# Sink rows on SP's queue and a later sink transposition in a windowed attention plus MLP mixer kernel

## The chip, the cores and the metric

The kernel runs on one core of one Trainium2 chip. The metric is device time in microseconds, the median of several runs: 228.32 us before the change (3 runs, 228.24 to 228.4).

## The reference

The first part is attention with sink tokens and a sliding window, over 4 batches, 8 heads, 768 positions and a head dimension of 64. Position `s` sees the first 4 keys (the sink rows) and the last 128 keys up to itself:

```
scores = scale * np.matmul(q, k.transpose(0, 1, 3, 2))
keep = is_sink | in_window          # pos < n_sink, or 0 <= rel < window
a = softmax(np.where(keep, scores, -1e9))
x = np.matmul(a, v)                 # heads joined to 512 channels
```

The second part is an MLP mixer over the result, first across tokens, then across channels:

```
h = np.maximum(xt @ w_tok1, 0.0) @ w_tok2     # xt: x with tokens last
u = x + h.transpose(0, 2, 1)
h2 = np.maximum(u @ w_ch1, 0.0) @ w_ch2
return u + h2
```

Inputs and output are float32. The kernel computes in bf16 with f32 accumulation.

## The kernel before

Heads are worked in pairs, 16 pairs in all, four to a batch. `load_qk` (L66) loads q and k of one pair in float32 with two DMAs on SP's queue, 384 KB each. `load_v` (L98) loads v of one pair with one DMA on POOL's queue that casts to bf16. `load_w` (L125) loads the weights on POOL's queue with a cast: `w_tok1`, `w_tok2`, and `w_ch1` and `w_ch2` in four parts each ("ch1" and "ch2" below).

For each pair the stages are these:

- `cast_qk` (L89) or, from pair 4 on, `cast` (L756) turn q and k into bf16 on POOL. Pair 0 is cast on DVE and ACT.
- `transpose_q` and `transpose_k` transpose on PE with six matmuls each (L111); the evictions to `qT` and to `kTz`, the two heads of k with zeros in the other half, go to DVE or ACT (L115, L117).
- `score(p, kt)`, six units of a pair, multiplies one block of 128 keys with two blocks of queries into PSUM, after a matmul that adds the mask (in batch 0). ACT takes the exponential (L438). For pair 0 each unit has one more matmul that only keeps TensorE busy (`keep_warm`).
- `score_sinks` does the same for the 4 sink rows, whose keys are in `kTs`, and `pv(p, half)` multiplies the probabilities with v and with the sink rows of v (`v_sink`). DVE takes the reciprocal of the sums (L491) and normalises into `x_sb` (L494).

Token mixing (`mix_h`, `mix_u`, `transpose_u`) follows each batch of four pairs, then channel mixing (`mix_channels`: `v1` units with `w_ch1`, `out_part` units with `w_ch2`).

Every instruction is issued in the order of the program, engine by engine (`in_order`), and an engine that waits at one instruction holds back what follows it. The order of the first stage is written by hand: SP issues q and k of pairs 0 to 3 (L130), and POOL issues, between L179 and L198, v of pair 0, the two sink loads of k, v of pair 1, the two sink loads of v, then the casts of pairs 1 and 2, v of pairs 2 and 3, the casts of pair 3, `w_tok1`, `w_tok2`, v of pair 4, the four parts of ch1 and v of pair 5 (L218 to L225). q and k of pair 4 wait on SP until `w_tok1` has landed, those of pair 5 until the second part of ch1 has landed.

The sink rows of batch 0 are loaded for all four pairs at once, one DMA for each head of the pairs (16 rows of 64 elements, 2 KB in bf16), into tiles that DVE has set to zero before; DVE also sets the column of ones of `v_sink` at the sink rows. `transpose_sinks` transposes `k_sink` on PE into `kTs`. It is the first unit behind `transpose_k` of pair 0. For later batches the sink rows come from `kTz` and `v`.

The order of everything else is set by `Plan.run` while the program is built. It keeps a clock for each engine, gives each unit a cost and each load a due time (the table `LANDED`, L765; for later loads the cost of a "Q" operation, that begins with 36500 ns, L778), and at each step appends the operation that can begin first. A main list (batch 0's attention, then the channel mixing of each batch) and a side list (the attention of the next batch) share PE. The casts of pair 4 and later, the loads of pair 6 and later (`load_pair`) and the loads of ch2 (`load_w2`) are placed by this plan too. `load_pair` and `load_w2` hand on `held`, the last load on POOL's queue: q and k of pairs 6 and 7 wait on SP until it has landed.

Of the kernel before, what the change touches and what calls it, by code (L numbers as in the profile page):

```python
# [9 lines left out]
FP32 = mybir.dt.float32  # L10
# [6 lines left out]
def kernel(  # L17
# [13 lines left out]
    nc = tc.nc  # L31
    B, H, S, D = q.shape
    P = 128
# [7 lines left out]
    NHP = H // 2  # L41
    HS = S // 2
    D1 = D + 1
    scale = 1.0 / float(D) ** 0.5

    singles = ctx.enter_context(tc.tile_pool(name="singles", bufs=1))
# [14 lines left out]
    in_order = tc.keep_in_program_order  # L61
# [4 lines left out]
    def load_qk(pidx, first=None):  # L66
        b, hp = pairs[pidx]
        h0 = 2 * hp
        raw = []
        for t, name in ((q, "q_f"), (k, "k_f")):  # L70
            f = raw_pool.tile([P, 2, NT, D], FP32, name=name)
            d = in_order(nc.sync.dma_start(
                out=f.rearrange("p h j d -> p h (j d)"),
                in_=t[b, h0:h0 + 2].rearrange("h (p j) d -> p h (j d)", j=NT),
            ))
            if first is not None:
                tc.add_manual_dep(
                    d.ins, first.ins.name,
                    mybir.DependencyInfo(mybir.DependencyClass.Sync, mybir.DependencyReason.DATA),
                    reason="transfers in the order in which they are needed",  # L80
                )
            raw.append(f)
        return raw
# [14 lines left out]
    def load_v(pidx):  # L98
        b, hp = pairs[pidx]
        v_aug = v_buf[pidx % NV]  # L100
        d = in_order(nc.gpsimd.dma_start(  # L101
            out=v_aug.rearrange("p i t d -> p (i t) d")[:, :, 0:D],
            in_=v[b].rearrange("h s d -> (h s) d")[2 * hp * S:2 * (hp + 1) * S].rearrange("(n p) d -> p n d", p=P),
        ))
        return v_aug, d
# [7 lines left out]
    def copy(e, out, in_):  # L113
        if e == "ACT":
            in_order(nc.scalar.activation(out, in_, AF.Copy))  # L115
        else:
            in_order({"DVE": nc.vector, "POOL": nc.gpsimd}[e].tensor_copy(out=out, in_=in_))  # L117
# [7 lines left out]
    def load_w(out, in_):  # L125
        return in_order(nc.gpsimd.dma_start(out=out, in_=in_))

    done = {}
    tiles = {}
    raws = {pidx: load_qk(pidx) for pidx in range(NHP)}  # L130
    vs = {}


# [3 lines left out]
    def keep_warm(n):  # L137
# [15 lines left out]
        out=ident, in_=ident, compare_op=ALU.not_equal, fill=1.0, base=0, pattern=[[-1, P]], channel_multiplier=1,  # L153
    ))
    for i in range(2):
        in_order(nc.gpsimd.affine_select(  # L156
            out=mask_main[:, i, 0], in_=mask_main[:, i, 0], compare_op=ALU.is_ge,
# [15 lines left out]
    v_sink0 = singles.tile([P, NHP, 2, D1], BF16, name="v_sink")  # L173
    v_sinks = [v_sink0[:, n] for n in range(NHP)]

    k_sink0 = singles.tile([P, NHP, 2, D], BF16, name="k_sink")
    in_order(nc.vector.memset(k_sink0, 0.0))
    in_order(nc.vector.memset(v_sink0, 0.0))
    vs[0], _ = load_v(0)  # L179
    for i in range(2):  # L180
        rows = slice(D * i, D * i + n_sink)
        in_order(nc.gpsimd.dma_start(  # L182
            out=k_sink0[rows, :, i], in_=k[0].rearrange("(p i) s d -> i s p d", i=2)[i, 0:n_sink],
        ))
    vs[1], _ = load_v(1)
    for i in range(2):
        rows = slice(D * i, D * i + n_sink)
        in_order(nc.vector.memset(v_sink0[rows, :, i, D:D1], 1.0))
        in_order(nc.gpsimd.dma_start(
            out=v_sink0[rows, :, i, 0:D], in_=v[0].rearrange("(p i) s d -> i s p d", i=2)[i, 0:n_sink],  # L190
        ))
    in_order(nc.vector.memset(kTz[0][D:P, 0], 0.0))
    in_order(nc.vector.memset(kTz[0][0:D, 1], 0.0))
    bfs = {0: cast_tiles()}
    cast_qk(1)
    cast_qk(2)
    vs[2], _ = load_v(2)
    vs[3], _ = load_v(3)  # L198

    w_tok1 = singles.tile([P, NT, DTOK], BF16)  # L200
# [15 lines left out]


    cast_qk(3)  # L218
    tok1_landed = load_w(w_tok1, moe_w_tok1.rearrange("(t p) n -> p t n", p=P))
    load_w(w_tok2, moe_w_tok2.rearrange("(t p) n -> p t n", p=P))  # L220
    raws[NHP] = load_qk(NHP, tok1_landed)
    vs[NHP], _ = load_v(NHP)
    ch1_landed = [load_ch1(n) for n in range(NW)]
    raws[NHP + 1] = load_qk(NHP + 1, ch1_landed[1])
# [18 lines left out]
    def landed(at):  # L243
        op = Op({}, None)
        op.done = at
        return op
# [92 lines left out]
    def unit(ns, fn, deps=(), tag=None, then=(), readers=None):  # L339
        op = Op({"PE": float(ns)}, fn, deps, tag, then, size=float(ns))  # L340
        for f in then:
            if op not in f.deps:
                f.deps.append(op)
        op.readers = list(then) if readers is None else readers
        return op
# [3 lines left out]
    def transpose_q(p):  # L349
        key = ("qT", p)  # L350

        def run():
            tiles["ps_q", p] = bank("mx", NT, P, dtype=BF16)
            for j in range(NT):
                transpose(tiles["ps_q", p][:, j], bfs[p][0][:, j])
            if p == 0:
                keep_warm(3)

        def evict(e):
            t = att_pool.tile([P, P, NT], BF16, name="qT2")  # L360
            copy(e, t, tiles["ps_q", p].rearrange("d j p -> d p j"))
            tiles[key] = t.rearrange("d p j -> d (p j)")

        done[key] = Op({"DVE": 950.0, "ACT": 900.0}, evict)
        done["tq", p] = unit(340, run, [done["q_bf", p]], "mx", [done[key]])
        return done["tq", p]
# [35 lines left out]
    def transpose_sinks():  # L402
        def run():
            ps = tiles["ps_ks"] = bank("mx", NHP, P, dtype=BF16)
            for n in range(NHP):
                transpose(ps[:, n], k_sink0[:, n].rearrange("p i d -> p (i d)"))

        op = Op({"ACT": 590.0, "DVE": 420.0}, lambda e: copy(e, kTs0.rearrange("p n i d -> p n (i d)"), tiles["ps_ks"]))
        for n in range(NHP):
            done["kTs", n] = op  # L410
        return unit(224, run, [landed(8000.0)], "mx", [op])

    def score(p, kt):
        nq = 2 if kt < NT - 1 else 1
# [222 lines left out]

    def attention_and_tokens(b):
        p0 = b * NHP
        units = [transpose_sinks()] if b == 0 else []  # L640
        units = [transpose_q(p0), transpose_k(p0)] + units
        for p in range(p0, p0 + NHP):
            more = p < p0 + NHP - 1
            units += [score(p, 0), score(p, 1)]
            if more:
                units.append(transpose_q(p + 1))
            if p > p0:
                units.append(pv(p - 1, 0))
            units += [score(p, 2), score(p, 3)]
            if more:  # L650
                units.append(transpose_k(p + 1))
            units.append(score(p, 4))
            if p > p0:
                units.append(pv(p - 1, 1))
            units += [score(p, 5), score_sinks(p)]

            if b:
                units[-1].then.append(sink_rows(p))
            if b and p == p0 + 2:
                units.append(mix_h(b, 0, 0, NTOK))  # L660
                units += [mix_u(b, 0, st, 2) for st in range(0, NT, 2)]
                plan.pending.append(transfer_u(b, 0, 0, NT, range(0, NT, 2)))
        if b == 0:
            units += [mix_h(b, 0, 0, 1), pv(p, 0), mix_h(b, 0, 1, 1), pv(p, 1)]
            units += [mix_u(b, 0, 0, 1, True), mix_u(b, 0, 1, 1), mix_h(b, 1, 0, NTOK), mix_u(b, 0, 2, 1, True)]
            units += [transpose_u(b, 0, 0, 1), mix_u(b, 0, 3, 1), transpose_u(b, 0, 1, 1)]
            units += [mix_u(b, 1, 0, 4), mix_u(b, 0, 4, 1, True), transpose_u(b, 0, 2, 1), mix_u(b, 1, 4, 2)]
            units += [mix_u(b, 0, 5, 1), transpose_u(b, 0, 3, 1), transpose_u(b, 0, 4, 1)]
            units += [transpose_u(b, 1, 0, 4), transpose_u(b, 1, 4, 2), transpose_u(b, 0, 5, 1)]
        else:  # L670
            units += [pv(p, 0), pv(p, 1), mix_h(b, 1, 0, NTOK)]
            units += [mix_u(b, 1, st, 2) for st in range(0, NT, 2)]
            plan.pending += [transfer_u(b, 1, 0, 4, (0, 2)), transfer_u(b, 1, 4, 2, (4,))]
        return units
# [81 lines left out]
    def cast(n, i, name):  # L756
# [7 lines left out]

    LANDED = {  # L765
        "q_bf": [0, 8400, 10500, 14700], "k_bf": [0, 9500, 12000, 15500],
        "v": [14700, 16300, 17800, 19200, 25000, 35500], "vs": [9500] * NHP,
        "raw": [0] * NHP + [26000, 36500],
    }
    for n in LANDED:  # L770
        for p in range(len(LANDED[n])):
            done[n, p] = landed(float(LANDED[n][p]))
    done["tok1"], done["tok2"] = landed(21100.0), landed(23000.0)
    for n in range(NW):
        done["ch1", n] = landed(27500.0 + 2000.0 * n)

    plan = Plan()
    plan.free.update(PE=3000.0, ACT=2200.0, DVE=3900.0, Q=36500.0)  # L778
# [15 lines left out]
    def pad_rest(e):  # L794
        in_order(nc.vector.memset(kTz[1][D:P, 0], 0.0))
        in_order(nc.vector.memset(kTz[1][0:D, 1], 0.0))

    done["masks"] = Op({"DVE": 1000.0}, mask_rest, [landed(4400.0)])
    done["pads"] = Op({"DVE": 760.0}, pad_rest, [done["k_bf", 0]])
    plan.pending += [done["masks"], done["pads"]]  # L800

    for n in range(NHP, len(pairs)):
        if n >= NHP + 2:
# [74 lines left out]
```

## Time and profile before

| | |
|---|---|
| median of 3 runs | 228.32 us (228.24 to 228.4) |
| the profiled execution | 229.29 us, of which the span is 227.6 us |
| mean granted clock of TensorE | 0.974 |
| PE, DVE, ACT, POOL busy | 93%, 57%, 51%, 23% of the span |
| DMA moved | 28.60 MB, mean 126 GB/s |

The profile was taken of one execution. All its times are counted from the start of the span. PE is TensorE, PEld its loading of weights, DVE the vector engine, ACT the scalar engine, POOL GpSimd and SP the engine that issues most DMAs. A line of a timeline gives the start, the duration, the engine, the line of the code, the operation, the tile written and the tile read, and in brackets how long the engine was idle before it and what ended that. A line of the chain gives the start and the length of one link of the chain of work that ended last, followed back from the last instruction. A line of the waits view gives who waited for whom, the microseconds in total, the number of times and the longest. "Landing" is the time from the issue of a DMA to its last byte.

### The profile page before, as it was taken

To read this page: it belongs to the slowest core of one execution; us is meant where nothing else is said; L and a number is where in the kernel's file an instruction comes from. 1 tells how busy PE (TensorE), PEld (TensorE's weight loads), DVE (VectorE), ACT (ScalarE), POOL (GpSimd) and SP (SyncE) were. 2 spreads that over 40 slices of the span, in tenths; PEclk is the share of its full clock that TensorE was granted. 3 is DMA by queue.
4 is the path that set the end of the run, shared out by engine and by line. 5 is a ranking of instruction groups with operands and counts; after the bars stand their busy time and mean duration, and the time that the engine had idled before them with its cause. 6 is when DMAs were issued, how large, how long until landed. Compare 5 with 4: busy or idle time off the path is not lost.

```text
span 227.6 us, 4342 instructions
## 1 busy us (share of the span) xinstructions
PE 210.6 (93%) x1738; PEld 135.6 (60%) x1756; DVE 130.3 (57%) x285; ACT 117.0 (51%) x233; POOL 52.5 (23%) x70
## 2 busy tenths in 40 slices
PE   7419989999999999999999999999999999999992
PEld 2216667777676665577766565567766654665440
DVE  7302776859866935379996735599939452000321
ACT  3304888689875710397891600689966110774000
POOL 7799023470474140230332000000000000000000
PEclk9956999999999999999999999999999999999998
DMA  6999999999999599480325514200003224100222
GB/s 182 322 172 152 224 226 182 209 157 169 313 347 132 122 287 196 156 277 5 25 16 57 137 50 108 99 4 0 3 0 70 94 78 129 49 0 0 92 92 94
DMA packets 51604, 28.60 MB, mean 126 GB/s; under 512 B 35712, under 2 KB 48512, under 8 KB 51584
## 3 DMA queue, kind: packets, MB, share of 16 engines
q0 software_dynamic: 29920, 7.09, 33.3%
q1 hardware_dynamic: 21664, 21.24, 30.2%
q8 instruction: 13, 0.21, 0.4%
q14 instruction: 7, 0.06, 0.1%
HBM read 26.76 MB, written 6.29 MB: 145 GB/s over the span
## 4 chain that ended last, share of the span: by engine, by line
PE 83%; DMA 5%; DVE 5%; ACT 3%; issue 2%; POOL 1%; ACTq 0%
PE ps_mx L108 64%; PE ps_sc L108 9%; PE ps_pv L108 5%; DMA k_sink<-in_k_dram 5%; PE ps_mx L111 5%; DVE kTz L117 2%; ACT kTz L115 1%; ACT pT L438 1%; DVE o_sb L710 1%; DVE x_sb L494 0%; POOL v_aug L101 0%; DVE qT L117 0%; DVE kTs L117 0%; POOL k_sink L182 0%; POOL mask_main L156 0%
## 5 line engine op out<-in xcount | busy, mean ns | idle before, releaser
L108 PE MATMUL ps_mx<-uT,w_ch 128*128 128x384 bf16 x384 | 69.8, 326 | 0.1
L108 PE MATMUL ps_mx<-w_ch,v1T 128*128 128x512 bf16 x274 | 65.0, 379 | 0.7
L438 ACT ACTIVATE pT<-ps_sc 128x512 bf16<-128x512 f32 x84 | 45.8, 567 | 24.1 <-PE ps_sc L108 23.1
L108 PEld LDWEIGHTS <-w_ch 128*128 128x128 bf16 x384 | 36.8, 98 | 20.8
L710 DVE TENSOR_TENSOR o_sb<-ps_mx,u_sb 128x512 f32<-128x512 f32 x24 | 16.5, 688 | 49.3 <-PE ps_mx L108 47.4
L108 PEld LDWEIGHTS <-v1T 128*128 128x128 bf16 x288 | 27.5, 98 | 28.5
L121 ACT ACTIVATE v1T<-ps_mx 128x384 bf16<-128x384 f32 x67 | 32.8, 491 | 18.1 <-DVE o_sb L710 9.8
L108 PE MATMUL ps_sc<-qT,kTz 128*128 128x256 bf16 x168 | 29.6, 268 | 2.3 <-DVE kTz L117 0.9
L444 DVE TENSOR_TENSOR pT<-pT,mask_main 128x512 bf16<-128x512 bf16 (+1 forms) x59 | 26.3, 457 | 1.0 <-ACT pT L438 0.5
L108 PEld LDWEIGHTS <-kTz 128*128 128x128 bf16 x192 | 17.8, 99 | 12.7 <-issue 2.0
L101 POOL DMA_DIRECT2D v_aug<-in_v_dram x16 | 16.6, 1039 | 23.9 <-PE ps_sc L108 12.0
L108 PEld LDWEIGHTS <-w_tok 128*128 128x128 bf16 x192 | 17.7, 98 | 5.6 <-issue 0.5
L123 DVE TENSOR_SCALAR v1T<-ps_mx 128x384 bf16<-128x384 f32 x29 | 16.0, 556 | 5.5 <-PE ps_mx L108 5.2
L117 POOL CAST q_bf<-q_f 128x768 bf16<-128x768 f32 x12 | 10.0, 830 | 36.8 <-DMA q_f<-in_q_dram 15.5
L117 DVE COPY qT<-ps_mx 128x768 bf16<-128x768 bf16 x13 | 12.4, 955 | 10.2 <-PE ps_mx L111 10.1
L108 PEld LDWEIGHTS <-pT 128*128 128x128 bf16 x352 | 16.8, 98 | 1.9
L595 DVE TENSOR_TENSOR u_sb<-ps_mx,x_sb 128x512 bf16<-128x512 f32 (+2 forms) x23 | 14.0, 655 | 6.3 <-PE ps_mx L108 6.2
L121 ACT ACTIVATE h1T<-ps_mx 128x512 bf16<-128x512 f32 (+2 forms) x9 | 4.9, 549 | 22.9 <-PE ps_mx L108 22.9
L115 ACT ACTIVATE kTz<-ps_mx 64x768 bf16<-64x768 bf16 x19 | 15.2, 801 | 2.6 <-PE ps_mx L111 1.8
L108 PE MATMUL ps_pv<-v_aug,pT 128*128 128x65 bf16 x304 | 16.2, 194 | 0.0
L494 DVE TENSOR_TENSOR x_sb<-ps_pv,recip 128x384 bf16<-128x384 f32 x28 | 15.5, 554 | 0.5
L117 DVE COPY kTz<-ps_mx 64x768 bf16<-64x768 bf16 x13 | 12.4, 955 | 1.7 <-PE ps_mx L111 1.3
(71 smaller groups left out, 198.3 us busy)
## 6 DMA issues: line engine op xcount, KB each, us to landing
q_f<-in_q_dram SPq DMA_DIRECT2D x16, 384.0 KB, 5.8
k_f<-in_k_dram SPq DMA_DIRECT2D x16, 384.0 KB, 6.4
out_dram<-o_sb SPq DMA_DIRECT2D x24, 256.0 KB, 2.0
v_aug<-in_v_dram POOLq DMA_DIRECT2D x16, 192.0 KB, 6.8
w_ch<-in_moe_w_ch_dram POOLq DMA_DIRECT2D x8, 384.0 KB, 8.7
w_tok<-in_moe_w_tok_dram POOLq DMA_DIRECT2D x2, 384.0 KB, 5.7
uT<-u_sb SPq DMA_TRANSPOSE x9, 3.2
k_sink<-in_k_dram POOLq DMA_DIRECT2D x2, 2.0 KB, 11.2
```

What stands on the lines that cost most here:

```text
L101: d = in_order(nc.gpsimd.dma_start(out=v_aug.rearrange("p i t d -> p (i t) d")[:, :, 0:D], in_=v[b].rearrange("h s d -> (h s) d")[2 * hp * ...
L108: in_order(nc.tensor.matmul(*args, skip_group_check=True, **kwargs))
L111: in_order(nc.tensor.transpose(out, in_, ident))
L115: in_order(nc.scalar.activation(out, in_, AF.Copy))
L117: in_order({"DVE": nc.vector, "POOL": nc.gpsimd}[e].tensor_copy(out=out, in_=in_))
L121: in_order(nc.scalar.activation(out, in_, AF.Relu))
L123: in_order(nc.vector.tensor_scalar_max(out=out, in0=in_, scalar1=0.0))
L438: in_order(nc.scalar.activation(tiles["pT", p][:, kt, :, 0:nq], tiles["ps_s", p, kt][:, :, 0:nq * P], AF.Exp, scale=scale,))
L444: in_order(nc.vector.tensor_tensor(out=pt, in0=pt, in1=msk[:, :, 0:nq], op=ALU.mult))
L494: in_order(nc.vector.tensor_tensor(out=x_sb[b][:, ts(half, QH), ts(hp, 2 * D)].rearrange("p t (i d) -> p t i d", i=2), in0=tiles["ps_o", p ...
L595: in_order(nc.vector.tensor_tensor(out=u_part(b, g, s0, n), in0=tiles["ps_u", b, g, s0], in1=x_sb[b][:, s0:s0 + n, c0:c0 + cn], op=ALU.add,))
L710: in_order(nc.vector.tensor_tensor(out=o_sb.rearrange("p (g c) -> p g c", g=2), in1=u_rows(b, st), in0=tiles["ps_out", b, st].rearrange("p ...
```

## The change

The sink rows are loaded in float32 on SP's queue. Two float32 tiles, `k_sink_f` and `v_sink_f`, are set to zero by DVE; the two loads of k's sink rows stand between the loads of q and k of pair 0 and those of pair 1, and the two loads of v's sink rows between pair 1 and pair 2. The ones of v's tile are set by DVE behind each of v's loads. Two new operations, placed by the plan on DVE or ACT, cast the tiles to bf16. POOL no longer issues sink loads. The unit `transpose_sinks` stands behind the fourth score unit of pair 0, just ahead of `transpose_k` of pair 1. The loads of q and k of pair 4 wait for v of pair 2 and no longer for `w_tok1`. Some due times of the plan are changed.

```diff
-    raws = {pidx: load_qk(pidx) for pidx in range(NHP)}
+    raws = {0: load_qk(0)}
...
+    sinks_f = [singles.tile([P, NHP, 2, w], FP32, name=f"{n}_sink_f") for n, w in (("k", D), ("v", D1))]
     k_sink0 = singles.tile([P, NHP, 2, D], BF16, name="k_sink")
-    in_order(nc.vector.memset(k_sink0, 0.0))
-    in_order(nc.vector.memset(v_sink0, 0.0))
+    for t in sinks_f:
+        in_order(nc.vector.memset(t, 0.0))
+    for t, f in zip((k, v), sinks_f):
+        for i in range(2):
+            rows = slice(D * i, D * i + n_sink)
+            in_order(nc.sync.dma_start(
+                out=f[rows, :, i, 0:D], in_=t[0].rearrange("(p i) s d -> i s p d", i=2)[i, 0:n_sink],
+            ))
+            if t is v:
+                in_order(nc.vector.memset(f[rows, :, i, D:D1], 1.0))
+        if t is k:
+            raws[1] = load_qk(1)
+    for p in range(2, NHP):
+        raws[p] = load_qk(p)
     vs[0], _ = load_v(0)
-    for i in range(2):
-        rows = slice(D * i, D * i + n_sink)
-        in_order(nc.gpsimd.dma_start(
-            out=k_sink0[rows, :, i], in_=k[0].rearrange("(p i) s d -> i s p d", i=2)[i, 0:n_sink],
-        ))
     vs[1], _ = load_v(1)
-    for i in range(2):
-        rows = slice(D * i, D * i + n_sink)
-        in_order(nc.vector.memset(v_sink0[rows, :, i, D:D1], 1.0))
-        in_order(nc.gpsimd.dma_start(
-            out=v_sink0[rows, :, i, 0:D], in_=v[0].rearrange("(p i) s d -> i s p d", i=2)[i, 0:n_sink],
-        ))
...
-    vs[2], _ = load_v(2)
+    vs[2], v_landed = load_v(2)
...
-    raws[NHP] = load_qk(NHP, tok1_landed)
+    raws[NHP] = load_qk(NHP, v_landed)
...
-        return unit(224, run, [landed(8000.0)], "mx", [op])
+        return unit(224, run, [done["k_sink"]], "mx", [op])
...
-        units = [transpose_sinks()] if b == 0 else []
-        units = [transpose_q(p0), transpose_k(p0)] + units
+        if b == 0:
+            sinks = transpose_sinks()
+        units = [transpose_q(p0), transpose_k(p0)]
...
             units += [score(p, 2), score(p, 3)]
+            if p == 0:
+                units.append(sinks)
...
-        "v": [14700, 16300, 17800, 19200, 25000, 35500], "vs": [9500] * NHP,
-        "raw": [0] * NHP + [26000, 36500],
+        "v": [14700, 16300, 17800, 19200, 25000, 38000],
+        "raw": [0] * NHP + [28500, 39000],
...
-        done["ch1", n] = landed(27500.0 + 2000.0 * n)
+        done["ch1", n] = landed(28500.0 + 2400.0 * n)
...
+    done["k_sink"] = Op({"DVE": 420.0, "ACT": 590.0}, lambda e: copy(e, k_sink0, sinks_f[0]), [landed(6800.0)])
+    v_sink = Op({"DVE": 420.0, "ACT": 590.0}, lambda e: copy(e, v_sink0, sinks_f[1]), [landed(8500.0)])
+    for n in range(NHP):
+        done["vs", n] = v_sink
...
-    plan.pending += [done["masks"], done["pads"]]
+    plan.pending += [done["masks"], done["pads"], done["k_sink"], v_sink]
```

More of the change, by code (lines that the diff above doesn't have):

```diff
@@ L218 @@
     cast_qk(3)
-    tok1_landed = load_w(w_tok1, moe_w_tok1.rearrange("(t p) n -> p t n", p=P))
+    load_w(w_tok1, moe_w_tok1.rearrange("(t p) n -> p t n", p=P))
     load_w(w_tok2, moe_w_tok2.rearrange("(t p) n -> p t n", p=P))
-    raws[NHP] = load_qk(NHP, tok1_landed)
+    raws[NHP] = load_qk(NHP, v_landed)
     vs[NHP], _ = load_v(NHP)
```

## The prediction, made before the result was known

> **What bounds the kernel now.** I read the page first, then the chain that ended last in order of time, then the busy time by stretch, and last the timelines of the engines in the first 66 us.
>
> ```profile
> PE 210.6 (93%) x1738; PEld 135.6 (60%) x1756; DVE 130.3 (57%) x285; ACT 117.0 (51%) x233; POOL 52.5 (23%) x70
> ...
> PEclk9956999999999999999999999999999999999998
> ...
> k_sink<-in_k_dram POOLq DMA_DIRECT2D x2, 2.0 KB, 11.2
> ```
>
> TensorE is busy for 93% of the span, so a gain must come from its idle 17 us or from its slow clock. The clock row has one dip, in slices 3 and 4 (5.7 us each). The last line is odd: 2 KB needed 11.2 us to land. The chain says what that costs:
>
> ```profile
> 4.20 0.78 POOL k_sink L182
> 4.97 10.99 DMA k_sink<-in_k_dram
> 15.96 0.14 issue
> 16.10 0.59 PE ps_mx L111 x4
> 16.69 0.85 PE ps_sc L108 x3
> ```
>
> From 4.97 to 15.96 the end of the kernel hangs on the sink rows of k. PE has nothing behind the 4 matmuls of k's transposition (8.36) until 16.10: 7.74 us, the only PE wait on a transfer in the first 45 us (the waits view: 7.7, once). The stretches show the second loss:
>
> ```profile
> 8.00:12.00 4.00, 0.36 (x2) 0.00 (x0) 0.00 (x0) 1.12 (x2) 2.49 (x4) 0.85 1.23 319
> 12.00:16.00 4.00, 0.00 (x0) 0.00 (x0) 0.00 (x0) 0.00 (x0) 4.00 (x5) 0.50 1.96 158
> 16.00:20.00 4.00, 3.90 (x19) 2.41 (x20) 0.50 (x2) 1.19 (x2) 4.00 (x6) 0.50 1.53 117
> 20.00:24.00 4.00, 3.73 (x24) 2.12 (x23) 2.66 (x3) 2.57 (x5) 2.93 (x4) 0.87 1.56 186
> ```
>
> The columns are PE, PEld, DVE, ACT, POOL, then granted clock, DMA share, GB/s. A mean of 0.85 over 4 us is 1.2 us at 0.5, so the clock fell at about 10.8, 2.4 us into the idle time; 0.87 puts its return at about 21.0, 4.9 us after work began again. Half of 4.9 is 2.5, so the stall and its slow clock are worth at most 7.7 + 2.5 = 10.2 us.
>
> **The main term.** I compare one event in both kernels: the first matmul of the first pv unit (pair 0, first half), at 25.07 before. It must wait for two things.
>
> First, PE's own progress. In the new order score units follow directly on the k transposition. They need kTz of pair 0, whose two ACT evictions end at 9.15. DVE gets longer memsets ahead of the q cast: 512 f32 in place of 256 uint32 elements (0.27 us; mask_main's 512 elements took 0.48), so +0.25 with v's being alike (520 elements, 0.49). First score: 9.4. From there I take the same stage of pair 1, which ran at full clock: first score matmul at 23.29, its pv at 29.71, 6.4 us, set by ACT and DVE rather than PE. Pair 0 has six extra warming matmuls (6 x 0.21) and the 4 sink transpositions (0.3), but no pv units of an earlier pair (0.36 + 0.45): +0.8 if PE set the pace, nothing if not. So 15.8 to 16.6.
>
> Second, v of pair 0. Issued at 3.05, it lands 12.4 us later, at 15.4, just behind the last SP load (k of pair 3, 4.41 + 10.3 = 14.7). SP's four new issues and their wait push that stream: the memset of the k tile ends at about 2.85, so q of pair 1 is issued at about 3.9 in place of 1.82. K of pair 0 landed at 5.0 and the stream had no break behind it; now q1's data starts 0 to 0.9 us late. I take 0.9, as q0 (issued 0.81, landed 3.0 later, over 1 us of that its own bytes) shows nearly 2 us ahead of its data. So v of pair 0 lands at 15.4 to 16.3.
>
> Both say 16.4 within half a microsecond: 25.07 - 16.4 = **8.7 us earlier**.
>
> Other parts of that stage. The casts of pair 1 (before at 8.62 and 9.64, POOL) end at 10.4 and 11.4; PE wants q after two score units (0.43 each, and 0.21 for the warming matmul), at 10.7, and k at 12.6: hidden. The sink rows of k, behind only q0 and k0, land at about 6 and are needed at 12.4; those of v, behind k1, at about 10.6. Each needs a cast f32 to bf16, 0.33 (q_bf: 768 elements, 0.49), on DVE, which is idle from 7.74 until the qT eviction at about 11. The cover for v's cast is thin: if v's rows land later than 10.8, DVE waits and the qT eviction slips by the same. POOL loses 1.37 + 1.15 us of issues, worth nothing, since its next work waits for q1.
>
> A rule of the Trainium skill weighs on the clock: "TensorE: Matmul & The Clock Gate", Part 1, says that about 3.4 us of sustained work release the clock, and its event list shows the throttle 5.2 us behind the last matmul. Here it was 4.9 and 2.4 us. By the page's figure the slow stretch would be worth 1.7 rather than 2.5 us, and the most to be had 9.4.
>
> **What is late next.** Shifted by 8.7, PE meets loads that had slack before. I compare each pair's q and k transposition less 8.7 with the end of its POOL casts.
>
> - Pair 4: 28.2 and 28.5. Its loads now wait for v of pair 2 (lands 18.6, plus 0.9) and not for tok1 (16.38 + 5.2 = 21.6). With the old 8.5 and 10.0 us to land they arrive at 28.0 and 29.6 and are cast by 28.8 and 30.4: up to 1.9 late. But the order is built with 28.5 as due time (26.0 before), so these 0.67 us of PE work stand further back, behind mixing units. I take 0.3; bounds 0 and 1.9.
> - Tok1 and tok2 share the engines with pair 4 sooner. At 21.6 and 23.5 they are wanted at 37.6 - 8.7 = 28.9 and 32.5: free.
> - Pair 5: wanted at 37.7 and 41.1, cast at 38.44 and 40.24. Its due time goes from 36.5 to 39.0: nothing.
> - Pair 6: 45.7 and 46.8, cast at 44.67 and 47.34: -1.0 to +0.5.
> - Pair 7: 56.4 and 57.6, cast at 60.47 and 61.43: **4.1 late** if its loads don't move.
>
> ```profile
> 37.62 0.83 POOL L117 CAST q_bf<-q_f 128x768 bf16<-128x768 f32 x1 [4.56 <-DMA q_f<-in_q_dram]
> 38.39 1.02 POOL L101 DMA_DIRECT2D v_aug<-in_v_dram  x1
> 39.40 0.84 POOL L117 CAST k_bf<-k_f 128x768 bf16<-128x768 f32 x1
> 40.17 1.50 POOL L126 DMA_DIRECT2D w_ch<-in_moe_w_ch_dram  x2
> ...
> 46.51 0.83 POOL L117 CAST k_bf<-k_f 128x768 bf16<-128x768 f32 x1 [1.84 <-DMA k_f<-in_k_dram]
> 47.28 1.52 POOL L126 DMA_DIRECT2D w_ch<-in_moe_w_ch_dram  x2
> 48.80 2.04 POOL L101 DMA_DIRECT2D v_aug<-in_v_dram  x2
> 59.64 0.83 POOL L117 CAST q_bf<-q_f 128x768 bf16<-128x768 f32 x1 [8.79 <-DMA q_f<-in_q_dram]
> ```
>
> This is POOL's queue. Pair 7 on SP waits for the last ch2 load (48.04 + 7.4 = 55.4), whose issue stands behind the cast of k6, whose load waits for v of pair 5 (21.85 + 17.7 = 39.6). With pair 5 due at 39.0 and the load queue still free at 36.5 in the plan, v6's issue moves ahead of both casts of pair 5, to about 31: v6 then fills the hole in the DMA before 40 (its share is 0.49 from 36 to 40, 1.31 after) and no longer shares the engines with q6 and k6. K6 took 6.3 us; k0 took 3.7 alone. So k6 lands 2 to 2.5 us earlier, and the last ch2 with it by about 2 (two ch2 loads take 1.9 us apiece, back to back), perhaps 3.5. Pair 7 is then 0.6 to 2.1 late; I take 0.8. Bounds: 0 and 4.1.
>
> Behind pair 7 every load has over 20 us in hand (pair 8: cast 63.28, used 94.27), and PE is busy to the end, so what is left of the shift at 60 us arrives at the end.
>
> **Sum:** 8.7 - 0.3 - 0.8 = 7.6 us. The profiled execution took 229.29 (span 227.6 and 1.7 around it) and becomes 221.7; the median of the runs is 228.32, 0.97 lower, and becomes **220.7**. About 0.2% (0.46 us) can be told from no change.
>
> **Rivals.**
>
> 1. Clean shift: v6's move and v of pair 2 make all loads early enough. 8.4 to 9.4 us: 218.9 to 219.9. For: both late loads get a head start. Against: the page's DMA row stands at 9 nearly all the way to 38 us, so little arrives sooner. 0.18.
> 2. Pair 7 becomes the bound: late by 1.8 to 4.1, gain 6.6 to 4.3, 221.7 to 224.0. If PE idles beyond 2.4 us there, the clock falls as at 10.8, for another 2.4: up to 226.4. For: 4.1 in the old chain. 0.20, a third of it above 224.
> 3. V of pair 0 later than 16.4: the POOL queue's packets hardly move while SP's queue is full (8 to 12 us: 0.08 MB against 1.20). At 19 the gain is 6.0 - 1.1: 223.4. 0.08.
> 4. It doesn't do what it says: the rows land no sooner, and PE waits as before, 228.3. Against: a 384 KB load issued on SP at 1.82 landed at 8.5, the 2 KB on POOL issued at 4.2 at 15.7. 0.03. "DMA: Bandwidth & Descriptors", "Issuing engines are not separate DMA queues", of the Trainium skill gives the reason for this one: all queues end on the same 16 engines and interleave, so the issuing engine only saves issue time. The 0.08 against 1.20 MB speak for very unequal shares.
> 5. Slower. The memsets of v's ones columns now stand behind v's sink load in the program, on the same tile. If they wait for its landing, DVE stops at 3.4 until about 10.6; kTz memsets (0.76) and the q cast follow, the cast at 11.4 instead of 4.19. From cast to first score took 5.0, so that comes at 16.4 to 17 against 16.48, at the low clock as before, with the SP stream 0.9 later and pv no earlier: about 229.0. It decides as soon as the wait exists. Against: the four ch1 loads write interleaved columns of one tile, and were issued at 18.9 to 21.1 though the first landed at 27.5; disjoint columns don't wait. 0.06.
>
> The forecast's own case (gain 6.6 to 8.4, 219.9 to 221.7) has 0.42; 0.03 is for anything else. Range 219.0 to 224.5: it leaves out part of rival 1's and 2's ends and rivals 4 and 5. Faster 0.91, same 0.03, slower 0.06.
>
> **What would show it.** K_sink landing in 2 to 4 us from SP; no PE wait between 9.4 and 16; one clock stretch, not two; first pv near 16.4; v6's issue on POOL ahead of pair 5's casts; a PE wait on POOL's cast of pair 7 near 57, under 2.4 us. A ones memset on DVE later than 4 us, a first pv behind 18, or a second fall of the clock would make it wrong.

## The result and the profile after

The median is 227.59 us (13 runs, 226.48 to 230.28); the kernel before, run beside it on the same chip, took 229.31 us (13 runs, 228.24 to 231.93). The ratio is 0.9931, 95% interval 0.9905 to 0.9957: 1.6 us faster, where 7.6 were forecast. The profiled execution took 227.7 us, its span 225.7 (227.6 before). Some executions of a kernel are over 1.5% slower than its fastest; the ratios leave them out, and the profiles of two experiments (pair 4 on `w_tok1` with new due times, fillers ahead of pairs 5 and 7) are of such executions and serve only to show what PE waits for.

Two lines of the page of the kernel after:

```profile
PEclk9999999699889999999999999999999999999998
...
PE 66%; DMA 18%; POOL 6%; DVE 4%; issue 2%; ACT 2%; SPq 1%; POOLq 0%
```

The dip of the clock is gone from slices 3 and 4. Slices 8 and 11 to 12, around 42 and 62 us, have new ones. The last line is the chain by engine: DMA still holds 18%.

The timelines of PE and DVE in the first stage say that the stall itself is gone:

```profile
10.32 0.86 DVE L117 CAST v_sink<-v_sink_f 128x520 bf16<-128x520 f32 x1 [1.52 <-DMA v_sink_f<-in_v_dram]
...
14.85 0.35 PE L108 MATMUL ps_pv<-v_aug,pT 128*128 128x65 bf16 x6
```

The first pv is at 14.85, against 25.07 before: 10.2 us sooner, 1.5 more than forecast. (The ten other runs with these loads in the first stage have it between 14.4 and 15.4.) The timeline of PE and the stretches at 40 and 60 us (columns as in the prediction) show where that went:

```profile
40.81 0.82 PE L111 MATMUL ps_mx<-ident,q_bf 128*128 128x128 bf16 x6 [2.70 <-POOL q_bf L117]
...
60.32 0.51 PE L111 MATMUL ps_mx<-ident,q_bf 128*128 128x128 bf16 x6 [2.49 <-POOL q_bf L117]
```

```profile
...
40.00:44.00 4.00, 3.19 (x21) 2.27 (x22) 1.69 (x2) 1.22 (x3) 2.40 (x4) 0.57 0.80 170
...
60.00:64.00 4.00, 3.68 (x31) 2.77 (x32) 1.75 (x4) 1.90 (x3) 3.77 (x6) 0.59 1.06 374
```

The first two lines are the q transpositions of pairs 5 and 7. PE waits 2.7 and 2.5 us for POOL's casts, and each wait brings a slow stretch: a mean of 0.57 over 4 us is 3.4 us at 0.5. Finer stretches put the two at 40.3 to 43.7, of which PE worked 2.9 us, and 60.7 to 64.1, of which it worked nearly all. Half of that time, 1.5 and 1.7 us, is what PE's work took longer there. Together: 10.2 - 2.7 - 2.5 - 1.5 - 1.7 = 1.8 us, and the span is 1.9 shorter. The sum leaves out smaller waits; the largest new one is 0.7 us for `x_sb` at 68.3.

The chain in order of time shows who made the two casts late:

```profile
20.99 12.44 DMA w_ch<-in_moe_w_ch_dram
...
33.97 8.27 DMA k_f<-in_k_dram
...
42.36 0.83 POOL k_bf L117
43.19 1.27 POOL w_ch L126 x2
...
47.22 7.24 DMA w_ch<-in_moe_w_ch_dram
...
54.47 4.85 DMA q_f<-in_q_dram
...
59.44 0.84 POOL q_bf L117
```

Pair 5's loads wait on SP for the second part of ch1, which lands at 33.43 (31.86 before). POOL issues ch1 1.3 us later than it did. POOL's timeline after and then before:

```profile
20.25 3.00 POOL L126 DMA_DIRECT2D w_ch<-in_moe_w_ch_dram  x4
```

```profile
18.91 3.00 POOL L126 DMA_DIRECT2D w_ch<-in_moe_w_ch_dram  x4
```

Ahead of ch1 on POOL's queue stand the casts of pairs 2 and 3, which wait for q and k, and SP now sends these later (q of pair 2 at 5.28, 2.84 before). The loads of pair 5 then run beside v of pairs 5 and 6 (landed at 41.1 and 42.9). Their q needs 6.3 us from issue to landing (5.5 before), their k 8.3 us (6.5 before). The cast of k5 holds back two issues of ch2 on POOL's queue, the last ch2 load goes out behind k6's cast, and pair 7's loads wait for it.

### The profile page after: what moved, and what is told of

It is laid out like the page before. It is cut to its first block, busy times and chain, and to the rows that moved or that the text cites. A ratio compares the mean times of both kernels' runs of the same rounds, so it can differ in the third digit from the quotient of the medians.

```text
span 225.7 us, 4340 instructions
## 1 busy us (share of the span) xinstructions
PE 211.1 (94%) x1738; PEld 135.5 (60%) x1756; DVE 132.4 (59%) x287; ACT 118.1 (52%) x233; POOL 50.5 (22%) x66
## 4 chain that ended last, share of the span: by engine, by line
PE 66%; DMA 18%; POOL 6%; DVE 4%; issue 2%; ACT 2%; SPq 1%; POOLq 0%
PE ps_mx L108 54%; DMA w_ch<-in_moe_w_ch_dram 9%; DMA k_f<-in_k_dram 7%; PE ps_sc L108 6%; PE ps_pv L108 4%; PE ps_mx L111 3%; DMA q_f<-in_q_dram 2%; DVE kTs L117 1%; POOL v_aug L101 1%; POOL w_ch L126 1%; ACT kTz L115 1%; POOL q_bf L117 1%; POOL k_bf L117 1%; POOL k_bf L92 1%; POOL w_tok L126 1%
## 5 line engine op out<-in xcount | busy, mean ns | idle before, releaser
L108 PE MATMUL ps_mx<-uT,w_ch 128*128 128x384 bf16 x384 | 71.9, 330 | 0.1
L121 ACT ACTIVATE v1T<-ps_mx 128x384 bf16<-128x384 f32 x68 | 33.3, 491 | 20.6 <-PE ps_mx L108 10.0
L108 PE MATMUL ps_sc<-qT,kTz 128*128 128x256 bf16 x168 | 30.6, 272 | 1.6 <-ACT kTz L115 0.9
L447 DVE TENSOR_TENSOR pT<-pT,mask_main 128x512 bf16<-128x512 bf16 (+1 forms) x59 | 27.5, 474 | 1.3 <-ACT pT L441 0.7
L108 PEld LDWEIGHTS <-pT 128*128 128x128 bf16 x352 | 17.1, 99 | 1.9
L123 DVE TENSOR_SCALAR v1T<-ps_mx 128x384 bf16<-128x384 f32 x28 | 15.4, 556 | 3.8 <-PE ps_mx L108 3.6
L117 DVE COPY qT<-ps_mx 128x768 bf16<-128x768 bf16 x12 | 11.4, 954 | 10.2 <-PE ps_mx L111 10.0
L121 ACT ACTIVATE h1T<-ps_mx 128x512 bf16<-128x512 f32 (+1 forms) x8 | 4.6, 571 | 23.2 <-PE ps_mx L108 23.2
L497 DVE TENSOR_TENSOR x_sb<-ps_pv,recip 128x384 bf16<-128x384 f32 x28 | 16.3, 582 | 0.4
L111 PE MATMUL ps_mx<-ident,q_bf 128*128 128x128 bf16 x96 | 8.6, 230 | 5.5 <-POOL q_bf L117 5.2
```

What stands on the lines that cost most here:

```text
L108: in_order(nc.tensor.matmul(*args, skip_group_check=True, **kwargs))
L111: in_order(nc.tensor.transpose(out, in_, ident))
L121: in_order(nc.scalar.activation(out, in_, AF.Relu))
L123: in_order(nc.vector.tensor_scalar_max(out=out, in0=in_, scalar1=0.0))
L447: in_order(nc.vector.tensor_tensor(out=pt, in0=pt, in1=msk[:, :, 0:nq], op=ALU.mult))
L497: in_order(nc.vector.tensor_tensor(out=x_sb[b][:, ts(half, QH), ts(hp, 2 * D)].rearrange("p t (i d) -> p t i d", i=2), in0=tiles["ps_o", p ...
```

## Experiments

Three theories. **Theory 1**: the two late pairs cost their waits and the slow clock behind them, so that freeing one load gives its part back. **Theory 2**: the pace and order of the transfers is the limit; freeing one load moves the wait to another. **Theory 3**: the changed due times, which reorder units and POOL's queue, cost the gain.

**Parts of the change.** First, the sink rows alone: pair 4 waits for `w_tok1` again, with the old due times (their lines are not shown).

```diff
-    raws[NHP] = load_qk(NHP, v_landed)
+    raws[NHP] = load_qk(NHP, tok1_landed)
```

> Only the sink rows' loads on SP and the later sink transposition; pair 4's loads wait for w_tok1 and the due times are those of before. Theory 1 (two late loads: the first pv comes 10.2 us sooner, and PE gives 5.2 us back in waits for the casts of pairs 5 and 7 and 3.4 us at the low clock behind them): the early gain is there in full (first pv near 14.9), waits of PE for q or k of pairs 4, 5 or 7 sum to 4 to 8 us, total 0 to 3 us faster than before. Theory 3 (the new due times and the order that they set cost the gain): with the old ones 6 to 8 us faster than before.

Measured: ratio 0.9997 (0.9974 to 1.0019). PE's longest wait:

```profile
PE ps_mx L111 <- POOL q_bf L117: 5.0, 1, 5.0
```

It is for q of pair 4 (its k costs 1.2 more), and the clock is at 0.5 from 31.2 to 38.0. The first pv comes at about 15.4 us and nothing is left of it: without earlier loads the stall only moves from 8 us to 27 us. SP's timeline has q of pair 5 here:

```profile
33.16 0.37 SPq L72 DMA_DIRECT2D q_f<-in_q_dram  x1
```

That is nearly as late as in the change (33.49; 31.92 before), though pair 4's loads go out at 22.90 and not at 18.91. So pair 4's earlier loads are not what delays pair 5. POOL issues ch1 at 20.22 here, as late as in the change.

With the new due times, but pair 4 on `w_tok1`:

> The changed kernel with pair 4's q and k on w_tok1 again (due times as changed). They are issued at about 23 in place of 18.9 and cast by 32 and 34; PE wants them at 29.6. A wait of 2 to 5 us for pair 4 with a low clock behind it; the wait for pair 5 shrinks by as much. Theory 1 and 2: 0.993 to 1.0, between the changed kernel and the sink part alone.

Measured: 0.9896 (0.9834 to 0.9958) in four runs from 225.2 to 230.9 us: too wide to place between the change and the sink rows alone. Its profile has waits of 3.3 and 1.3 us for pair 4, as expected, and 2.1 for pair 7.

The whole change with the old due times:

> The changed kernel with the due times of before; pair 4's loads wait for v of pair 2. PE comes to pair 4 at about 27, 2 us ahead of the cast of its k, a wait of 1 to 2.5 us there; the loads of v of pair 6 come behind the cast of pair 5's q again, so pair 5 lands sooner and pair 7 later. Theory 2: 0.993 to 1.0. Theory 3 (the new due times cost the gain): 0.975 to 0.985.

Measured: 0.9909 (0.9876 to 0.9943), which overlaps the change's own interval. PE waits 1.6 us for k of pair 4, 2.0 for pair 5, and 0.6 ahead of q of pair 7, which the profile puts down to ACT. Theory 3 falls: due times shift waits between the pairs, but do not set the sum.

The queue alone: the transposition goes back to its old place, right behind k of pair 0.

```diff
-        units = [transpose_q(p0), transpose_k(p0)]
+        units = [transpose_q(p0), transpose_k(p0)] + ([sinks] if b == 0 else [])
...
-            if p == 0:
-                units.append(sinks)
```

> The changed kernel with the sink transposition directly behind k of pair 0, as before. If the queue alone takes the wait of 7.7 us away: k's sink rows land and are cast by 9, PE waits for them under 1 us, first pv at 15 to 16, and the total is that of the changed kernel, 0.990 to 0.997. If the later transposition is needed as well: a PE wait of 2 us or more at the sink transposition.

Measured: 0.9942 (0.9921 to 0.9964), first pv near 15.5, a wait of 0.5 us for the cast of k's sink rows. SP's queue alone takes the stall away. What the later place adds is not told apart: the first pv lies just beside the 14.4 to 15.4 of the runs that have it, and the interval overlaps the change's.

The later transposition alone, in the kernel before:

> The kernel before with only the sink transposition moved behind four score units; the sink rows stay on POOL's queue, with the loads and due times of before. They land at about 15.8 again, so PE waits from about 11.5 to 15.9, 4.4 us in place of 7.7, and first pv comes 2 to 4 us sooner than before. Theory 1 and theory 2 both say that most of that is lost at pair 4, whose loads don't move (the kernel with the sink part alone gained nothing from 9.5 us): 0.995 to 1.005. If a small shift is kept: 0.985 to 0.99.

Measured: 0.988 (0.9851 to 0.9909), outside the main expectation, within the alternative (a small shift is kept), and no worse than the whole change. Its waits:

```profile
PE ps_mx L111 <- DMA k_sink<-in_k_dram: 5.1, 1, 5.1
...
PE ps_mx L111 <- POOL q_bf L117: 0.3, 1, 0.3
```

The first pv is at 21.7, only 3.4 us sooner, but no later load is missed by more than 0.3 us: 2.7 us are kept of 3.4, against 1.6 of 10.2.

**The slow clock.** Ten matmuls that only keep TensorE busy (`mm(filler, ones[:, 0:P], ones)`) ahead of the q transpositions of pairs 5 and 7:

> The changed kernel with ten matmuls on constants (2.1 us) ahead of the q transpositions of pairs 5 and 7, where PE waits 2.7 and 2.5 us; their result is not used. Theory 1: the waits end when they did, the idle time shrinks to 0.6 us, the clock stays at full speed behind both, and 2 to 3.4 us go: ratio to before 0.978 to 0.985. If the low clock costs nothing, because the stage behind it is bound by ACT and DVE: no change against the changed kernel (0.993).

Measured: 0.9936 (0.9903 to 0.9968), as the change. In its profile neither dip is there, but the transposition of pair 7 starts no sooner (60.24, 60.32 in the change): what the clock saves behind pair 5 is spent waiting for pair 7's loads. What it saves behind pair 7 goes as well: PE waits 2.2 us for `x_sb` until 68.10, where the change waits 0.7 until 68.31, and the clock falls at 69.3 instead.

**Freeing a load.** Pair 7's loads wait for v of pair 6 and no longer for ch2:

```diff
-            nonlocal held
-            held = load_ch2(n)
+            load_ch2(n)
```

> The changed kernel, with q and k of pair 7 waiting for v of pair 6 (landed 42.9) and no longer for the last ch2 load (54.5). PE's order stays. Theory 1: pair 7 is cast before 52, the wait at 57.8 and the low clock behind it go, 2.5 + 1.7 = 4.2 us: ratio to before 0.973 to 0.978. Theory 2 (the DMA's pace as a whole sets when pairs 5 to 7 can run, so a repair only moves the wait): a wait for pair 6, for ch2 or for a later pair takes its place, ratio above 0.988.

Measured: **0.9737** (0.971 to 0.9765), 222.42 us. The only load still waited for is pair 5's:

```profile
PE ps_mx L111 <- POOL q_bf L117: 2.2, 1, 2.2
```

As theory 1 has it. Now pair 5's loads on v of pair 4 instead:

```diff
-    vs[NHP], _ = load_v(NHP)
+    vs[NHP], v4_landed = load_v(NHP)
...
-    raws[NHP + 1] = load_qk(NHP + 1, ch1_landed[1])
+    raws[NHP + 1] = load_qk(NHP + 1, v4_landed)
```

> The changed kernel, with q and k of pair 5 waiting for v of pair 4 (landed 29.7) and no longer for the second ch1 load (33.4). PE's order stays. Theory 1: pair 5 lands 3 to 4 us sooner, the wait at 38.1 and its low clock go, and PE reaches pair 7 up to 4.4 us sooner, where the wait grows by that much unless its loads move too: 0 to 2 us better than the changed kernel, ratio to before 0.985 to 0.993. Theory 2: no better, with a wait at ch1 or pair 6 instead.

Measured: 1.0008 (0.9985 to 1.003). Theory 1 misses and theory 2's mechanism shows. POOL's timeline in this kernel:

```profile
37.33 0.83 POOL L117 CAST k_bf<-k_f 128x768 bf16<-128x768 f32 x1 [1.38 <-DMA k_f<-in_k_dram]
38.10 1.50 POOL L126 DMA_DIRECT2D w_ch<-in_moe_w_ch_dram  x2
46.81 0.82 POOL L117 CAST q_bf<-q_f 128x768 bf16<-128x768 f32 x1 [7.21 <-DMA q_f<-in_q_dram]
```

Pair 5's casts end at 35.9 and 38.2 and PE no longer waits for them. But POOL is free sooner, issues two ch2 loads at 38.1 (43.13 in the change), and these run beside q and k of pair 6: q needs 6.0 us from issue to landing, 3.2 in the change. PE waits 2.7 us for pair 6 and 6.0 for pair 7, with the clock at 0.5 from 59.7 to 66.5. Both edits together:

> Both releases at once: pair 5's q and k wait for v of pair 4, pair 7's for v of pair 6; PE's order is that of the changed kernel. Theory 1 (each late load is a wait of its own): pair 5's wait and its low clock go too, 2.3 + 1.7 = 4 us beyond the kernel with pair 7's release alone (0.974): 0.955 to 0.962. Theory 2 (a load that comes sooner frees POOL, which sends the next ch2 loads sooner, and these slow pair 6): no wait at pairs 5 and 7, but PE waits 2 to 3 us for pair 6 near 45, as with pair 5's release alone: 0.970 to 0.980.

Measured: 0.9793 (0.975 to 0.9837), as theory 2 has it and no better than pair 7's edit alone. The wait is now at pair 6, 2.9 us, and its q again needs 6.0 us. So the ch2 loads, which nobody needs yet, were placed behind pair 7's loads, on top of pair 5's edit:

```diff
-        if n == 2 * NHP - 2:
+        if n == 2 * NHP - 1:
```

> Pair 5's q and k wait for v of pair 4, and the four ch2 loads are issued behind pair 7's loads rather than ahead of them, so that pair 7 waits for v of pair 6 and no ch2 transfer runs beside pairs 5 and 6. The plan sets PE's order anew from there on (pair 7 a little sooner). Theory 1: no PE wait over 1 us at pairs 5, 6 and 7, no low clock behind the start, 0.950 to 0.965. Theory 2: the wait moves on, to ch2 near 60 or to pair 8, 0.970 or more.

Measured: **0.9721** (0.9695 to 0.9746), 222.17 us. POOL's timeline there, and PE's waits:

```profile
38.47 0.83 POOL L117 CAST k_bf<-k_f 128x768 bf16<-128x768 f32 x1 [1.36 <-DMA k_f<-in_k_dram]
...
45.87 0.88 POOL L117 CAST q_bf<-q_f 128x768 bf16<-128x768 f32 x1 [5.61 <-DMA q_f<-in_q_dram]
...
47.59 1.50 POOL L126 DMA_DIRECT2D w_ch<-in_moe_w_ch_dram  x2
```

```profile
PE ps_pv L108 <- DVE x_sb L497: 0.9, 1, 0.9
PE ps_mx L111 <- POOL q_bf L117: 0.8, 1, 0.8
```

No wait behind the start reaches 1 us, the clock row has no dip, and q of pair 6 needs 4.0 us. The interval lies below that of both edits together, so the ch2 transfers beside pair 6 are shown to cost. But the ratio misses theory 1's 0.950 to 0.965 and is not told apart from pair 7's edit alone (0.9737): waits for DVE (0.9 us for `x_sb`, 0.7 for `v_sink`) now stand beside that for pair 6. Pair 6 on the last part of ch1 as well:

> The kernel with ch2 behind pair 7 (0.972), with q and k of pair 6 waiting for the last ch1 load (40.0) rather than v of pair 5 (41.7). Its one PE wait for a load is 0.8 us for pair 6. Theory 1: that goes, 0.966 to 0.971. Theory 2: q and k of pair 6 share the engines with v of pairs 5 and 6 and land no sooner: 0.970 to 0.975.

Measured: 0.9669 (0.9623 to 0.9714), 221.77 us. That is theory 1's number without its mechanism: pair 6 still costs 0.9 us, and the interval overlaps the one before it, so it is not shown to be better. And the free pair 7 with ten filler matmuls ahead of pair 5:

> The kernel with pair 7's loads on v of pair 6 (0.974; its one wait of PE left is 2.25 us for pair 5, with 3.4 us at the low clock behind it and no late load after that), plus ten matmuls on constants ahead of pair 5's q transposition; their result is not used. If the low clock costs half of its time where no later load takes the gain back: 1.7 us less, 0.964 to 0.969. If it costs nothing, as the warm kernel with both waits seemed to say: 0.972 to 0.976.

Measured: 0.973 (0.9699 to 0.9762), no gain on 0.9737. PE's timeline:

```profile
88.59 0.48 PE L108 MATMUL ps_mx<-uT,w_ch 128*128 128x384 bf16 x2 [1.46 <-DMA uT<-u_sb]
```

The clock stays at 1.00, and from pair 5's to pair 7's q transposition it takes 15.5 us where 17.1 were needed; PE then waits 1.5 us for a transposing DMA of token mixing, 8.7 us after its issue (4.9 without the fillers). The 1.6 us are worked out as saved and seen as lost again. The kernel without the fillers agrees: of its six executions three had a mean clock of 1.0 and took 221.84 to 222.84 us, and three had 0.992 and took 222.25 to 222.61.

Last, the edits of pair 5 and ch2 in the kernel before (sink rows and pair 4 as they were):

> The kernel before, sink rows and their wait untouched, with only the load order of the 0.972 kernel: pair 5's q and k on v of pair 4, ch2 behind pair 7. If the loads pay only because PE comes sooner (in the kernel before, no wait for q or k behind the start): 0.993 to 1.002, with first pv at 25 as before. If they pay by themselves, so that the 0.972 is theirs and the sink part adds nothing: 0.970 to 0.985.

Measured: 0.9975 (0.9956 to 0.9994), with the stall where it was:

```profile
PE ps_mx L111 <- DMA k_sink<-in_k_dram: 7.5, 1, 7.5
```

Sinks alone (0.9997) and loads alone (0.9975) add up to 0.3%; together, with pair 4's earlier release, they give 2.8%. Neither pays alone. Pair 4's earlier release is in the whole and in neither part, and no run has it with the loads alone.

## Why the prediction was right or wrong

- **The stall and the slow clock behind it**: right in mechanism, 10.2 us where 8.7 were worked out. Both paths to the first pv were put too late. PE's first score unit began at 7.99, where 9.4 was taken, and its pv came 6.9 us behind it (6.4 to 7.2 were taken). V of pair 0 was put at 15.4 to 16.3 and landed at 10.2 (3.05 + 7.1), so it held nothing back. The stream on SP has a gap behind its four new issues and their wait for the memsets: from 4.4 to 5.4 us the DMA moves 55 to 134 GB/s, then 300 and more up to 6.2. From 6 us on POOL's queue moves. The DMA view from 5 to 12 us, packets, MB and share, of the kernel after and then before:

```profile
q0 software_dynamic: 2683, 0.34, 75.7%
q1 hardware_dynamic: 1014, 1.43, 66.3%
```

```profile
q1 hardware_dynamic: 1448, 2.10, 95.4%
q0 software_dynamic: 632, 0.08, 17.5%
```

  POOL's queue (q0) moved 0.34 MB where it had moved 0.08. The prediction took the gap as a delay for SP alone and did not ask who gains from it. That the gap is the cause is read from the order of events; no run has it alone. Rival 3 bet on the opposite sign.
- **Sink casts**: right, but for their price. DVE waited 1.5 us for v's rows, until 10.3, and its cast took 0.86 us where 0.33 was taken. The qT eviction, whose matmuls had ended at 10.2, began at 11.1, the time that the prediction had for it.
- **Pair 4** (0.3): close. Cast by 29.41, used at 29.57: no wait.
- **Pair 5** ("Its due time goes from 36.5 to 39.0: nothing"): this step failed. It took the cast times of the kernel before, 38.44 and 40.24. The 0.9 us by which it moved SP's stream were carried on to v of pair 2, but not through POOL's casts to ch1 and so to pair 5. Q was cast by 40.76 and PE was there at 38.12, a wait of 2.7 us: 1.6 from the later landing of ch1, 0.8 from the longer transfer of q, and 0.3 because PE came sooner than even the old cast. The due time places the units in order, but PE reached them sooner than that. With 1.5 us of slow clock pair 5 took 4.2 us, where nothing was put. K was cast by 43.19, without a wait of PE.
- **Pair 7** (0.8, bounds 0 and 4.1): this term was mis-sized, 2.5 + 1.7 us. Its q was cast by 60.27, only 0.2 us sooner than before (60.47): the last ch2 landed 1 us sooner (54.45 against 55.44), where 2 were taken, and q's own transfer, 4.9 us in place of 4.1, gave most of that back. Had pair 5 been on time, PE would have come here sooner and waited longer: the run that releases pair 5 alone has a wait of 6.0 us here, and no gain. That is rival 2; it priced a fall of the clock, but only for one pair and as an addition. The time lies beyond its 226.4 because pair 5 came on top.
- **V6 ahead of pair 5's casts**: foreseen (29.35, "about 31"), but oversold. Issued 9 us sooner, v of pair 6 landed only 0.8 us sooner (42.9, 43.7 before), and k of pair 6 1.0 sooner (45.4, 46.4 before), where 2 to 2.5 were taken. What it does to pair 5, whose k it ran beside, was not asked.
- **The change does not do what it says**, and **DVE held by the memsets of ones**: neither occurred; the memsets began at 3.46 us.
- **The clock**: a fall was forecast beyond 2.4 us of idle time, lasting 4.9 us of work. Here it fell 2.2 and 2.9 us after the idle time began, the second time when PE had been at work again for 0.4 us, and lasted 3.4 us. "TensorE: Matmul & The Clock Gate" of the Trainium skill, Part 1, puts one window of its activity monitor at about 3.4 us, and the length of both stretches agrees. The 5.2 us after the last matmul in its event list is not what these waits show. The traces show two things more. The slow stretches looked at last 3.4 us or a multiple: 6.8 behind the waits of 5.0 and 6.0 us (31.2 to 38.0, 59.7 to 66.5) and 10.2 before the change (10.8 to 21.0). And no one length of wait decides: the clock fell behind a wait of 2.0 us (old due times, at 40.0) and did not behind one of 2.7 (pair 5 on v of pair 4, at 47.7).

The forecast added terms that were each read off the old trace. What stays open is why k of pair 5 needs 8.3 us. With v of pair 6 issued only at 39.80 (old due times) it landed by 40.8, in 7.4 us or less. But with v of pair 6 issued ahead of its landing, at 34.55 (pair 4 on `w_tok1`) and at 28.48 (the queue alone), it took 6.5 and 7.0. So v of pair 6 alone does not explain it.

## What to carry to other kernels

When a stall early in a kernel goes, every later load that was hidden behind it has to be re-timed with the new neighbours it runs beside, not only shifted; here 8.4 of 10.2 us went back to two loads that had slack before. A queue that carries casts and DMA issues in order turns each landing into the release of the next transfer, so freeing one load can start one that nobody needs yet beside one that is urgent. Here about 2% came from letting the late load (pair 7) no longer wait for the unneeded one (ch2), by either of two edits (0.9737 and 0.9721); hurrying pair 5 alone gained nothing. Keeping the clock up with filler work was worth nothing here, where a transfer or another engine set the next wait.

## What the runs showed of the hardware

Operations of DVE in SBUF, even tiny copies, grew long while POOL worked beside them. In the kernel after, DVE's timeline:

```profile
65.81 2.43 DVE L117 COPY kTs<-kTz 128x8 bf16<-128x8 bf16 x1
```

and POOL's beside it:

```profile
65.58 0.83 POOL L117 CAST k_bf<-k_f 128x768 bf16<-128x768 f32 x1
66.36 1.01 POOL L101 DMA_DIRECT2D v_aug<-in_v_dram  x1
67.37 0.84 POOL L117 CAST q_bf<-q_f 128x768 bf16<-128x768 f32 x1
```

The copy ends at 68.24, POOL's second cast at 68.21. The mean of the kTs copy is 0.34 us over 5 of them in the kernel before and 0.68 over 6 in the one after. PE waited 0.7 us behind the long one, for `x_sb`. Behind its wait of 2.2 us in the kernel with fillers at pairs 5 and 7 stand two mask multiplications of DVE that took 4.09 us together (mean 0.46 each in the change), again beside casts of POOL. That POOL's work is the cause is argued from the overlap alone; no run took it away.
